# Which weight slices a recurrent loop streams, a copy in two parts, and one matmul group in another place

## The chip, the core and the metric

The kernel runs on one core of a Trainium2 chip. The metric is the device time of one execution in microseconds (us). All figures come from the profile and the trace of one profiled execution, or from the times of three further runs.

The engines, by the profile's names: PE does matmuls (PEld is its weight load), DVE and ACT are the vector and scalar engines, POOL is GpSimd, SP issues DMAs. ACT issues DMAs too. SBUF is the on-chip memory, PSUM holds what PE accumulates.

## The reference, cut to what matters

Two mixers read the same input x (2048 x 640) and a gate g adds them. A is a recurrent attention: x is cut into 64 segments of 32 rows, and each segment is joined with 8 memory rows that come out of the segment before it.

```python
for s in range(n_seg):                                  # 64 passes
    h = jnp.concatenate([mem, xs], axis=1)              # 8 + 32 rows, 640 wide
    q, k, v = (einsum('btd,dhe->bhte', h, W) for W in (Wq, Wk, Wv))   # 32 heads of 192
    p = softmax(where(mask, q @ k * scale, -1e9))
    o = einsum('bhte,hed->btd', p @ v, Wo)
    mem = o[:, :M, :]                                   # goes into the next pass
    outs.append(o[:, M:, :])
...
return g * a + (1 - g) * b
```

B is a local attention with a dilated window of 8 keys; it has its own projections. Each of Wq, Wk, Wv and Wo holds 640 x 6144 numbers in bf16, and every pass of A multiplies with all of them.

## The kernel before, in words

The work runs in four stages. Mixer B comes first (0 to about 190 us). The prepass (`prepass`, about 190 to 356 us) projects, for all 64 segments at once, the eight rows of x that the loop needs beside the memory, and writes them to a DRAM scratch. The loop (`part_a`, about 356 to 1660 us) makes the 64 passes, since the memory of one pass is an input of the next. `part_z` (to the end) finishes the remaining rows.

**Resident and streamed weights.** The four matrices do not all fit in SBUF. They are cut into slices of 384 KB. For Q, K and V a slice is named (matrix, u, kc): kc is one of five blocks of 128 rows of the 640, u one of three rounds of 512 columns, and it holds the columns of three of the four column groups (the fourth group is always resident). For Wo, "oa" is the first 384 output columns, in 12 slices, and "ob" the other 256, in 8 slices. `STREAM` (line 15) names the 14 slices that are not resident. They are copied once to a DRAM scratch `wscr`, and each pass reads all 14 from there, with `get_unit` (line 565), which issues the DMA of line 569 on SP. The tile pool of these slices, `wst`, has `WBUFS` = 5 buffers, which are used in turn. So the DMA of a slice is issued as soon as the last matmul with the slice five places before it has been done, and the slices come in the order in which the pass uses them. I write k03 for ("k", 0, 3), oa2 for ("oa", 2), and so on.

**Order in a pass.** The order of PE, ACT and DVE in the loop is written out by hand (a manual schedule, from line 956 on). `m_qk(i, kcs)` projects Q (i even) or K (i odd) of round i // 2 with the blocks kcs, `m_v(u, kcs)` projects V of round u (all at line 769); each block is four matmuls, one for each column group. `c_qk` copies a projection out of PSUM on ACT (line 782), `c_v(u)` copies V of round u on DVE into `VU[u]` (line 878). `t_qk` and `c_t` transpose. `s_a`, `s_b`, `e_exp`, `e_mask` (line 845), `e_norm` (line 855), `e_recip` make the softmax, for two halves h of the heads. `pv_half(h)` multiplies with V (lines 894 and, for the eight prepass rows `Vz`, 899); `Vz` is loaded in every pass by `load_vz` on ACT's queue (line 754). `c_x` and `c_z` copy the result (lines 908 and 915). `o_group(part, i2)` is one group of four matmuls with Wo (line 937); there are 12 groups of "oa" and 12 of "ob" in a pass.

`VU[1]` is columns 512 to 1024 of the tile `TZ`, while `pv_half` reads V in four tiles of 384 columns: `V[0]` 0 to 384, `V[1]` 384 to 768, `V[2]` 768 to 1152. So `pv_half(0)`, which reads `V[0]` and `V[1]`, needs `VU[0]` and the first half of `VU[1]`; the second half belongs to `V[2]` and is read by `pv_half(1)`.

**The end of a pass.** After `pv_half(1)` and its copies come six groups of ob (0 to 5), six of oa (6 to 11), a copy of the oa result on ACT (`whi`, line 1027), `load_z(s + 1)`, and six groups of ob (6 to 11). Behind ob group 8, `sel("oa", ...)` (line 948) multiplies that copy with a selection matrix, and DVE puts the result (line 951) into the next pass's `hT`, from which its first projection reads. So the next pass waits for the chain: last oa group, `whi`, `sel`, `hT`.

Of the kernel before, what the change touches and what calls it, by code (L numbers as in the profile page):

```python
# [11 lines left out]
F32 = mybir.dt.float32  # L12
I32 = mybir.dt.int32

STREAM = (("k", 0, 0), ("k", 0, 3), ("k", 1, 0), ("q", 2, 1), ("q", 2, 3), ("k", 2, 4), ("v", 0, 1), ("v", 1, 1), ("v", 2, 2),
          ("oa", 0), ("ob", 0), ("oa", 2), ("oa", 8), ("ob", 7))
N_EARLY = 21
N_COPY = 4
N_MID = 4
N_V = 8  # L20
# [2 lines left out]
WBUFS = 5  # L23
# [6 lines left out]
class _K:  # L30
# [463 lines left out]
    def units(self, m, J, kc):  # L494
        return [u for u in range(3) if J == 3 or (m, u, kc) not in STREAM]

    def weights_setup(self):
        nc, tc, KC = self.nc, self.tc, self.KC
        rest = []
        for m in "qkv":  # L500
            ks = sorted(range(KC), key=lambda kc: (len(self.units(m, 0, kc)) < 3, kc)) if m == "k" else range(KC)
            rest += [(m, J, kc) for kc in ks for J in range(4)]
        rest += [k for k in [("oa", i) for i in range(12)] + [("ob", i) for i in range(8)] if k not in STREAM]
        n = (0, N_EARLY, -N_MID - N_V - N_LAST, -N_V - N_LAST, -N_LAST, None)
        self.early, *self.late = [rest[n[x]:n[x + 1]] for x in range(5)]
# [5 lines left out]
        self.wstream = self.ctx.enter_context(tc.tile_pool(name="wstream", bufs=WBUFS))  # L511
        self.wscr = dict(zip(STREAM, self.dram.tile([len(STREAM), 128, 1536], BF, name="wscr")))

# [58 lines left out]
    def load_early(self):  # L572

        loads = [lambda k=k: self.load_res(k, self.tile_of(self.wres, k)) for k in self.early]
        self.pre_q = {}
        self.pre_keys = sorted((k for k in STREAM if k[0] in ("q", "k")), key=lambda k: (k[0] != "q", k[1]))
        loads += [lambda k=k: self.pre_q.update({k: self.load_unit(k)}) for k in self.pre_keys[:WBUFS]]
        loads += [lambda k=k: self.copy_unit(k) for k in STREAM[:N_COPY]]
        return loads
# [10 lines left out]
    def prepass(self):  # L590

        nc, tc, KC = self.nc, self.tc, self.KC
        nseg = self.S // self.seg
        NZ = nseg * 8
        self.zpk_dram = self.dram.tile([nseg, 128, 1152], BF, name="zpk_dram")

        def project_qk(p, pool):
            m, Rp = "qqkk"[p], p % 2
            ZS = pool.tile([128, nseg, 192], BF, name="ZS")
            if p == 2:  # L600
                for k in self.pre_keys[WBUFS:]:
                    self.pre_q[k] = self.load_unit(k)
            sts = {k: t for k, t in self.pre_q.items() if k[0] == m and k[1] in (2 * Rp, 1)}

            def weights(j, kc, l):
                key = (m, l // 4, kc)
                if j < 3 and key in sts:
                    return sts[key][:, 512 * j + 128 * (l % 4):512 * j + 128 * (l % 4) + 128]
                return self.res(m, j, kc, 128 * l, 128)

            if p == 2:
                for k in STREAM[N_COPY:]:
                    self.copy_unit(k)
            if p == 3:
                self.load_late(1)
            z0 = 768 + 192 * (1 - Rp) if m == "q" else 384 + 192 * Rp
            for r in range(2):
                for j in range(4):
                    for t in range(3):
                        ps = self.pst([128, NZ], F32, name="ps_pre")  # L620
                        for kc in range(KC):
                            nc.tensor.matmul(ps[:], lhsT=weights(j, kc, 6 * Rp + 3 * r + t), rhs=zTi[:, kc, :],  # L622
                                             start=(kc == 0), stop=(kc == KC - 1))
                        zc = 96 * r + 8 * (4 * t + j)
                        self.evac(ZS[:, :, zc:zc + 8], ps[:].rearrange("p (i s) -> p s i", i=8))
                        if p == 0 and 12 * r + 3 * j + t >= 6 and self.tail_outs:
                            self.tail_outs.pop(0)()
            nc.scalar.dma_start(self.zpk_dram[:, :, z0:z0 + 192].rearrange("s p f -> p s f"), ZS[:])

        vkeys = [k for k in STREAM if k[0] == "v"]  # L630

        def load_v(J):
            t = self.wstream.tile([128, 1536], BF, name="wst", tag="wst")
            for x, (m, u, kc) in enumerate(vkeys):
                nc.sync.dma_start(t[:, 512 * x:512 * x + 512],
                                  self.W["v"][:, kc, 1536 * J + 512 * u:1536 * J + 512 * u + 512])
            return t

        def project_v(vt, J):

            def weights(kc, g):
                if J < 3 and ("v", g, kc) in vkeys:
                    x = vkeys.index(("v", g, kc))
                    return vt[:, 512 * x:512 * x + 512]
                return self.res("v", J, kc, 512 * g, 512)

            for st in range(NZ // 128):
                ZV = zvp.tile([128, 1536], BF, name="ZV")
                pss = [self.pst([128, 512], F32, name="ps_pre") for _ in range(3)]
                for kc in range(KC):  # L650
                    for g in range(3):
                        mm = nc.tensor.matmul(pss[g][:], lhsT=zTi[:, kc, 128 * st:128 * st + 128],  # L652
                                         rhs=weights(kc, g), start=(kc == 0),
                                         stop=(kc == KC - 1))
                if 4 * J + st >= 3 and loads:
                    tc.add_manual_dep(loads.pop(0)().ins, mm.ins.name, self.after, reason="a load per tile")
                for g in range(3):
                    self.evac(ZV[:, 512 * g:512 * g + 512], pss[g][:])
                for k in range(2 * st, 2 * st + 2):
                    dst = self.zpk_dram[:, 32 * J + k:32 * J + 32:8, 0:384]  # L660
                    nc.scalar.dma_start(dst, ZV[64 * (k % 2):64 * (k % 2) + 64, :].rearrange("s (j f) -> s j f", j=4))

        zTi = self.zTi
        with ExitStack() as zc1:
            with tc.tile_pool(name="pre_zs0", bufs=1, reuse_waits="tile") as zs0:
                project_qk(0, zs0)
                self.out_ctx.close()
                zs1 = zc1.enter_context(tc.tile_pool(name="pre_zs1", bufs=1, side="right", reuse_waits="tile"))
                project_qk(1, zs1)
                project_qk(2, zs0)  # L670
            project_qk(3, zs1)
        vs = [load_v(J) for J in range(3)]
        loads = self.load_late(2, "right", wait=True)
        with tc.tile_pool(name="pre_zv", bufs=ZVB, reuse_waits="tile") as zvp:
            for J in range(4):
                project_v(vs[J] if J < 3 else None, J)
        for k in STREAM[:WBUFS]:
            self.ahead[k] = self.get_unit(k)

# [38 lines left out]
    def part_a(self):  # L718
        nc, tc, KC, S = self.nc, self.tc, self.KC, self.S
# [3 lines left out]
        with ctx:  # L723
# [3 lines left out]
            VU = [self.TZ[:, 512 * u:512 * u + 512] for u in range(3)]  # L727
# [33 lines left out]
            for s in range(nseg):  # L761
# [108 lines left out]
                pvs = {}  # L870
# [4 lines left out]
                    project(pvs[u], "v", u, kcs)  # L875

                def c_v(u):
                    nc.vector.tensor_copy(VU[u], pvs[u][:])  # L878

                def pv_half(h):  # L880
                    E = Es[h]
# [61 lines left out]
                def sel(part, hT_next, pm):  # L943

                    m0, m1 = (0, 3) if part == "oa" else (3, KC)
                    p = 0 if part == "oa" else 1
                    for m in range(m0, m1):
                        nc.tensor.matmul(pm[:, p, 8 * (m - m0):8 * (m - m0) + 8], lhsT=whi[:, m * 128:(m + 1) * 128],  # L948
                                         rhs=self.sel_m[:], start=(m == m0), stop=(m == m1 - 1),
                                         skip_group_check=True)  # L950
                    nc.vector.tensor_copy(hT_next[:, m0:m1, 0:8], pm[:, p, 0:8 * (m1 - m0)].rearrange(  # L951
                        "p (m i) -> p m i", i=8))
# [32 lines left out]
                e_mask(0)  # L985
                m_v(0)
                c_v(0)
                if s + 1 < nseg:
                    hT_next = self.load_seg(s + 1)
# [30 lines left out]
                nc.scalar.dma_start(self.oz_dram[s], zst)  # L1020
                if s + 1 == nseg:
                    self.sort_oz(0)
                for i2 in range(6):
                    o_group("ob", i2)
                for i2 in range(6, 12):
                    o_group("oa", i2)
# [1 line left out]
                if s + 1 < nseg:  # L1028
                    load_z(s + 1)
                    pm = psS.tile([128, 2, 512], F32, tag="S", name="ps_mem")  # L1030
                for i2 in range(6, 12):
                    o_group("ob", i2)
                    if i2 == 8 and s + 1 < nseg:
                        sel("oa", hT_next, pm)
# [135 lines left out]
```

## Time and profile before

| what | us |
|---|---|
| median of three runs (lowest, highest) | 1726.15 (1721.16, 1727.09) |
| the profiled execution, its own time | 1727.22 |
| its span in the trace | 1725.5 |
| PE busy in the span | 1608.7 |
| loop, 356 to 1660 us: PE busy of 1304 us | 1234.65 |
| from the first `c_v` of one pass to that of the next: mean of 63 | 20.41 |
| the same, shortest and longest | 19.25, 23.36 |

The granted clock of PE was 0.987 over the span. The times are to be read as one execution's: the work of a pass is the same in all 64 passes, so what differs between a pass of 19.25 us and one of 21 us is waiting. A matmul of the loop's projections has a mean duration of 380 ns in the list of groups, but such matmuls overlap, and four of them (one block) start every 206 to 216 ns; a wait of PE is therefore best read from the starts.

### The profile page before, as it was taken

What the parts mean: (1) busy time and instruction counts of PE and PEld (TensorE: products, weight loads), DVE (VectorE), ACT (ScalarE), POOL (GpSimd) and SP (SyncE); (2) the same over time, 40 slices, a digit from 0 to 9 for tenths busy, and PEclk for the clock granted to TensorE, in tenths of its full rate; (3) what the DMA queues carried; (4) which work ended last, traced back from release to release, by engine and by line L of the source; (5) the groups of instructions that cost most, each with busy time, mean ns of one, the idle gap of its engine ahead of it and who ended that gap; (6) DMA issues with size and microseconds to landing.
All of it is one profiled execution on the core that took longest, in us unless ns stands there. A gap on an engine that the chain in (4) does not pass through costs nothing.

```text
span 1725.5 us, 75561 instructions
## 1 busy us (share of the span) xinstructions
PE 1608.7 (93%) x33193; PEld 893.1 (52%) x33209; DVE 693.0 (40%) x2095; ACT 805.3 (47%) x2082; POOL 59.8 (3%) x124
## 2 busy tenths in 40 slices
PE   7887999999999999999999999999999999999989
PEld 4545544445555555555555555555555555555557
DVE  3666333234443343344443343444333443434430
ACT  3877322234444444444444444454444444444450
POOL 2030000000000000000000000000000000000000
PEclk9999899999999999999999999999999999999999
DMA  7888798989998998899999998999999998999981
GB/s 196 199 208 210 233 325 212 266 273 295 298 306 299 311 318 292 285 294 296 293 295 306 309 315 291 289 307 303 301 298 306 291 302 283 294 292 294 298 288 31
DMA packets 306391, 479.04 MB, mean 278 GB/s; under 512 B 100492, under 2 KB 184460, under 8 KB 306060
## 3 DMA queue, kind: packets, MB, share of 16 engines
q1 hardware_dynamic: 206928, 417.73, 75.1%
q10 hardware_dynamic: 99132, 56.46, 11.4%
q8 instruction: 260, 4.26, 1.0%
q14 instruction: 71, 0.58, 0.1%
HBM read 432.37 MB, written 47.23 MB: 278 GB/s over the span
## 4 chain that ended last, share of the span: by engine, by line
PE 71%; DMA 21%; ACT 2%; issue 2%; SPq 1%; DVE 1%; ACTq 0%; DVEq 0%
PE ps_qk L769 17%; DMA wst<-wscr 15%; PE ps_v L769 11%; PE ps_wo L937 11%; PE ps_pre L622 6%; PE ps_qkT L790 5%; PE ps_S L823 4%; PE ps_oT L894 4%; PE ps_pre L652 3%; PE ps_z L1101 2%; DMA TZ<-zpk_dram 2%; PE ps_S L855 2%; PE ps_bqk L236 1%; DMA bqkT<-bqk_dram 1%; PE ps_bo L360 1%
## 5 line engine op out<-in xcount | busy, mean ns | idle before, releaser
L769 PEld LDWEIGHTS <-hT 128*32 128x32 bf16 x11520 | 280.6, 96 | 311.8 <-issue 45.2
L782 ACT CAST TZ<-ps_qk 128x512 bf16<-128x512 f32 x384 | 219.7, 586 | 348.4 <-PE ps_qk L769 344.1
L769 PE MATMUL ps_qk<-w_q,hT 128*32 128x512 bf16 x3456 | 272.8, 382 | 1.5 <-issue 1.5
L769 PE MATMUL ps_qk<-w_k,hT 128*32 128x512 bf16 x3072 | 262.6, 380 | 0.0
L801 DVE COPY ZB<-ps_qkT 128x512 bf16<-128x512 bf16 (+1 forms) x256 | 90.9, 355 | 384.6 <-PE ps_qkT L790 284.2
L769 PE MATMUL ps_v<-w_v,hT 128*32 128x512 bf16 x3264 | 242.1, 381 | 0.0
L937 PEld LDWEIGHTS <-TZ 128*32 128x32 bf16 x6144 | 149.1, 96 | 94.5 <-ACT TZ L908 33.4
L769 PE MATMUL ps_qk<-wst,hT 128*32 128x512 bf16 x1152 | 150.0, 381 | 25.6 <-DMA wst<-wscr 24.2
L878 DVE CAST TZ<-ps_v 128x512 bf16<-128x512 f32 x192 | 132.8, 691 | 37.4 <-PE ps_v L769 37.3
L937 PE MATMUL ps_wo<-w_oa,TZ 128*32 128x384 bf16 x2304 | 136.6, 330 | 6.4 <-issue 5.0
L908 ACT CAST TZ<-ps_oT 128x192 bf16<-128x192 f32 x256 | 75.8, 322 | 136.6 <-PE ps_oT L899 76.0
L937 PE MATMUL ps_wo<-wst,TZ 128*32 128x384 bf16 (+1 forms) x1536 | 127.6, 306 | 2.5 <-issue 1.6
L937 PE MATMUL ps_wo<-w_ob,TZ 128*32 128x256 bf16 x2304 | 107.0, 274 | 9.0 <-issue 8.8
L908 DVE CAST TZ<-ps_oT 128x192 bf16<-128x192 f32 x256 | 85.7, 355 | 71.4 <-PE ps_oT L899 69.6
L951 DVE CAST hT<-ps_mem 128x24 bf16<-128x24 f32 x126 | 22.5, 178 | 216.3 <-PE ps_mem L948 216.3
L790 PE MATMUL ps_qkT<-ident,TZ 128*128 128x128 bf16 x1536 | 108.2, 221 | 0.0
L790 PEld LDWEIGHTS <-TZ 128*128 128x128 bf16 x1536 | 89.3, 98 | 21.6 <-issue 21.6
L841 ACT ACTIVATE TZ<-ps_S 32x224 bf16<-32x224 f32 x256 | 89.0, 348 | 9.6
L841 ACT ACTIVATE ZB<-ps_S 32x224 bf16<-32x224 f32 x256 | 89.0, 348 | 8.8
L750 POOL COPY TZ<-ZB 128x384 bf16<-128x384 bf16 x64 | 32.5, 507 | 1492.8 <-DMA ZB<-zpk_dram 783.5
L823 PE MATMUL ps_S<-ZB,TZ 64*128 64x160 bf16 (+1 forms) x768 | 82.2, 233 | 0.0
L894 PEld LDWEIGHTS <-TZ 32*128 32x128 bf16 (+1 forms) x4096 | 46.9, 97 | 63.0 <-issue 27.1
(133 smaller groups left out, 2042.6 us busy)
## 6 DMA issues: line engine op xcount, KB each, us to landing
wst<-wscr SPq DMA_DIRECT2D x896, 384.0 KB
zpk_dram<-ZS ACTq DMA_DIRECT2D x4, 3072.0 KB
ZB<-zpk_dram ACTq DMA_DIRECT2D x64, 192.0 KB
zpk_dram<-ZV ACTq DMA_DIRECT2D x32, 192.0 KB
TZ<-zpk_dram ACTq DMA_DIRECT2D x64, 96.0 KB
oz_dram<-TZ ACTq DMA_DIRECT2D x64, 96.0 KB
w_q<-in_A_Wq_dram SPq DMA_DIRECT2D x14, 384.0 KB
w_v<-in_A_Wv_dram SPq DMA_DIRECT2D x14, 384.0 KB
```

The lines of the kernel that those rows point to most:

```text
L622: nc.tensor.matmul(ps[:], lhsT=weights(j, kc, 6 * Rp + 3 * r + t), rhs=zTi[:, kc, :], start=(kc == 0), stop=(kc == KC - 1))
L652: mm = nc.tensor.matmul(pss[g][:], lhsT=zTi[:, kc, 128 * st:128 * st + 128], rhs=weights(kc, g), start=(kc == 0), stop=(kc == KC - 1))
L769: nc.tensor.matmul(ps[32 * j:32 * j + 32, :], lhsT=hT[:, kc, :], rhs=rhs, start=(kc == 0), stop=(kc == KC - 1), tile_position=(0, 32 * j), ...
L782: nc.scalar.copy(sts[i], pqs[i][:])
L790: nc.tensor.transpose(pT[:, 128 * t:128 * t + 128], st[:, 128 * t:128 * t + 128], self.ident[:])
L801: nc.vector.tensor_copy(QTf[:, run[2]:run[2] + 4, run[3]:run[3] + n, :].rearrange("p b x i -> p x b i"), src.rearrange("p (x b i) -> p x b ...
L823: nc.tensor.matmul(grid(h, par)[:, :, 0:80].rearrange("p j (b r i) -> p j b r i", r=2, i=8)[:, :, :, r, :], lhsT=KTs[3 * R + t][k0:k1, :], ...
L841: nc.scalar.activation(E[ps], pSs[h][ps, :, 112 * j:112 * j + 112], ACT.Exp, scale=scale_a)
L878: nc.vector.tensor_copy(VU[u], pvs[u][:])
L894: nc.tensor.matmul(out[:, r, t, :], lhsT=V[2 * h + r][ks, f0:f1], rhs=E[ks, par, 0:80].rearrange("p (b r i) -> p b r i", r=2, i=8)[:, :, r ...
L908: cp(oTxs[2 * h + j // 2][:, 6 * (j % 2):6 * (j % 2) + 6, :], pos[j][:, 0:240].rearrange("p (c q) -> p c q", q=40)[:, :, 8:40])
L937: nc.tensor.matmul(pso[part][32 * jj:32 * jj + 32, 0:n], lhsT=oTxs[2 * (g // 2) + J // 2][:, 6 * (J % 2) + 3 * (g % 2) + t, :], rhs=osl[pa ...
```

## The change

Three edits in the loop, and what follows from them ahead of it.

1. `STREAM` names other slices: ten of Q, K, V and four of Wo, where it was nine and five. The size of what a pass streams, 14 slices of 384 KB, and the five buffers stay. One more resident slice of Q, K, V or Wo is loaded early (`N_EARLY` 22 for 21). With four streamed slices of V instead of three, the prepass loads V's streamed columns in two tiles for each column group (`load_v`), one of three slices and one of one: six tiles in all, five ahead and the sixth after the first group has been projected.
2. `c_v(1)` copies `VU[1]` in two parts of 256 columns.
3. ob group 5 moves from ahead of oa groups 6 to 11 to behind them (and behind `whi` and `load_z`).

```diff
-STREAM = (("k", 0, 0), ("k", 0, 3), ("k", 1, 0), ("q", 2, 1), ("q", 2, 3), ("k", 2, 4), ("v", 0, 1), ("v", 1, 1), ("v", 2, 2),
-          ("oa", 0), ("ob", 0), ("oa", 2), ("oa", 8), ("ob", 7))
-N_EARLY = 21
+STREAM = (("k", 0, 2), ("q", 1, 1), ("k", 1, 2), ("q", 2, 1), ("q", 2, 4), ("k", 2, 4), ("v", 0, 0), ("v", 1, 0), ("v", 1, 3),
+          ("v", 2, 2), ("oa", 0), ("ob", 0), ("oa", 5), ("ob", 7))
+N_EARLY = 22
...
-        def load_v(J):
+        def load_v(J, n):
             t = self.wstream.tile([128, 1536], BF, name="wst", tag="wst")
-            for x, (m, u, kc) in enumerate(vkeys):
+            for x, (m, u, kc) in enumerate(vkeys[3 * n:3 * n + 3]):
...
-        vs = [load_v(J) for J in range(3)]
+        vs = [(J, n) for J in range(3) for n in range((len(vkeys) + 2) // 3)]
+        vts = [load_v(*v) for v in vs[:WBUFS]]
...
             for J in range(4):
-                project_v(vs[J] if J < 3 else None, J)
+                project_v([t for v, t in zip(vs, vts) if v[0] == J], J)
+                vts += [load_v(*v) for v in vs[len(vts):]]
...
                 def c_v(u):
-                    nc.vector.tensor_copy(VU[u], pvs[u][:])
+                    for f0, f1 in ((0, 256), (256, 512)) if u == 1 else ((0, 512),):
+                        nc.vector.tensor_copy(VU[u][:, f0:f1], pvs[u][:, f0:f1])
...
-                for i2 in range(6):
+                for i2 in range(5):
                     o_group("ob", i2)
                 for i2 in range(6, 12):
                     o_group("oa", i2)
...
-                for i2 in range(6, 12):
+                for i2 in range(5, 12):
                     o_group("ob", i2)
                     if i2 == 8 and s + 1 < nseg:
                         sel("oa", hT_next, pm)
```

More of the change, by code (lines that the diff above doesn't have):

```diff
@@ L643, in weights @@
                     x = vkeys.index(("v", g, kc))
-                    return vt[:, 512 * x:512 * x + 512]
+                    return vt[x // 3][:, 512 * (x % 3):512 * (x % 3) + 512]
                 return self.res("v", J, kc, 512 * g, 512)
```

## The prediction

> **What bounds the kernel.** I read the page's engine shares first, then the loop's windows, then PE's waits in the loop, then single passes in the timeline.
>
> ```profile
> PE 1608.7 (93%) x33193; PEld 893.1 (52%) x33209; DVE 693.0 (40%) x2095; ACT 805.3 (47%) x2082; POOL 59.8 (3%) x124
> ...
> q1 hardware_dynamic: 206928, 417.73, 75.1%
> ```
>
> PE is busy almost throughout, and q1, SP's queue with the streamed slices, takes three quarters of the DMA engines' time. Either could be the bound, so passes have to be compared.
>
> ```profile
> 551.83:571.08 19.25, 18.98 (x449) 10.56 (x445) 8.23 (x29) 9.71 (x28) 0.51 (x1) 1.00 0.92 314
> 390.14:1653.00 1262.86, 1199.58 (x27594) 661.87 (x27590) 511.21 (x1737) 603.01 (x1736) 31.44 (x62) 1.00 0.91 299
> ```
>
> These are the windows of one short pass and of 62 passes (length, busy time of PE, PEld, DVE, ACT, POOL, clock, DMA share, GB/s). The short pass takes 19.25 us at 314 GB/s, the mean pass 20.37 us at 299 GB/s with the same work. So the transfers can go faster than they do on average, and some 1.1 us of a mean pass is waiting. PE's waits in the loop say for what (us in total, times, longest):
>
> ```profile
> PE ps_qk L769 <- DMA wst<-wscr: 24.2, 35, 2.0
> ...
> PE ps_mem L948 <- ACT ZB L1027: 14.7, 57, 0.5
> ...
> PE ps_oT L899 <- DMA TZ<-zpk_dram: 1.4, 5, 0.4
> ```
>
> The first row is projections that wait for a streamed slice, the second the selection that waits for the copy `whi`. Each row counts only idle time after the modelled end of the matmul before. That end is 379 ns after its start, while the next block can start after 206, so each slice wait hides another 0.17 us: 24.2 + 35 x 0.17 = **30 us** for the slices.
>
> **Edit 1, other slices: -23 us.** A buffer is refilled when the slice five places before has been used, so a slice's lead is the time from that use to its own. I took the median gap between each two neighbouring PE starts of the 62 inner passes, which gives a pass without waits (19.22 us), and read from it when each slice is used. Before, the leads are in us: k00 5.3, k03 5.0, k10 5.8, q21 6.3, q23 6.8, k24 7.1, v01 7.4, v11 8.1, v22 8.2, oa0 8.1, ob0 8.6, oa2 7.5, oa8 6.0, ob7 5.8. Five uses (ob0, oa2, oa8, ob7, k00) lie 0.66 to 1.08 us apart, so five refills are issued almost at once. Packets of one slice take 1.05 us at best and 1.3 to 1.9 us in most places, so these refills queue up: from issue to first packet it is about 0.8 to 1.7 us at k00, k03, k10 and oa8, but 2.3 at q21 and 3.2 at k24. Placing each wait by its slice (start over the usual 206 ns), q21 waits in 26 passes for 15 us, k03 in 12 for 7, k10 in 7 for 6.5, q23 in 4 and k24 in 3 for 2.5 and 1.7 us; the slices with leads from 7.4 us up hardly at all.
>
> With the new list, the same pass without waits gives: k02 7.5, q11 7.4, k12 6.95, q21 6.9, q24 7.0, k24 6.4, v00 6.55, v10 6.35, v13 7.3, v22 6.4, oa0 6.8, ob0 7.0, oa5 6.8, ob7 6.7. The shortest lead grows from 5.0 to 6.35 us, and no more than two uses in a row are under 1 us apart (0.86 to 0.88), so the queue stays at about one slice. Such slices resemble the old oa8 and ob7 (leads 6.0 and 5.8, short queue: one wait in 62 passes and none) more than the old q21. I take one wait of 0.5 us in 62 passes for each of 14 slices, 7 us, so 30 - 7 = 23 us go. Bounds: all 30 go, or (as at k24, with a lead of 7.1 and a long queue) 3 waits of 0.57 for each of 14, 24 us, and only 6 go.
>
> Outside the loop this edit adds three loads of 128 KB in the prepass and one early load of 384 KB. In the prepass PE runs matmul after matmul (107.7 us busy of 110 between 190 and 300 us), and none of its waits there is for these tiles. The sixth V tile is loaded on SP behind the first column group, some 20 us ahead of its use; behind it on SP stand Wo loads and the refills for the loop, which have 12 us of the last group as cover. I cost it at nothing; without the cover it is 0.8 MB at 273 GB/s, 3 us.
>
> **Edit 2, the copy in two: -7 us.** One pass in the timeline:
>
> ```profile
> 901.25 0.69 DVE L878 CAST TZ<-ps_v 128x512 bf16<-128x512 f32 x1 [0.62 <-PE ps_v L769]
> ...
> 901.78 0.42 PE L894 MATMUL ps_oT<-TZ 32*128 32x40 bf16 x16
> 901.86 0.27 DVE L845 TENSOR_TENSOR ZB<-ZB,mask 128x224 bf16<-128x224 bf16 x1
> ...
> 902.39 0.28 PE L855 MATMUL ps_S<-ZB,bones 128*32 128x160 bf16 x8
> ```
>
> The 16 matmuls of L894 are one group on the page's line, but their starts have a hole: twelve from 901.78 to 901.86, the last four (columns 640 to 768, of `VU[1]`) at 902.00, which is 901.94, the copy's end, and 0.06 us. Over all passes this hole is 147 ns where the neighbours have 15 to 29. The slope between the 192-column copy of L908 (355 ns) and the 512-column one (691 ns) is 1.05 ns a column, so half the columns take 267 ns less, and the first half ends about 424 ns after its start, at 901.67, before PE comes. So about 0.12 us a pass goes. What else becomes late: `e_mask` stands behind the copy on DVE. The next instruction starts 0.61 us after a 512-column copy, so 0.08 us of the 0.69 overlaps; two halves then hold DVE for 2 x (424 - 80) = 688 ns, 78 more. The mask would end at 902.21 instead of 902.13, and L855, which needs it, would come at 902.27 instead of 902.39: just in time with 0.06 us for the signal. 64 x 0.12 = 7.7 us, bounds 8.4 (all of 0.13) and 3 (the mask is late by 0.07).
>
> [...]
>
> **Edit 3, ob group 5 behind: -5 us.**
>
> ```profile
> 907.22 0.51 PE L937 MATMUL ps_wo<-w_ob,TZ 128*32 128x256 bf16 x12
> ...
> 907.45 0.48 ACT L1027 CAST ZB<-ps_wo 128x384 bf16<-128x384 f32 x1 [1.44 <-PE ps_wo L937]
> ...
> 907.99 0.23 PE L948 MATMUL ps_mem<-sel_m,ZB 128*128 128x8 bf16 x3 [0.26 <-ACT ZB L1027]
> ```
>
> After the three ob groups PE waits for `whi`: from the last group's start to L948 it is 528 ns in the median, where an ordinary change of this kind takes about 100 to 310. An ob group takes 108 ns (starts of neighbouring groups). Put into this wait it is free, and the chain from oa's end on starts 108 ns earlier. Ahead of oa 6, however, one cover group is missing: oa 6 reads the first ACT copy of `c_x(1)`, which ended at 905.29 in this pass; oa 6 started at 905.40 and now wants 905.29, and would be released at about 905.34. So 0.06 to 0.11 us a pass; 63 x 0.08 = 5 us, bounds 3.5 and 6.8. No DMA is moved past another by it; `load_z` is issued 0.1 us earlier.
>
> **Vz: +3 us.** `load_vz` is issued about 9.0 us into the pass on ACT's queue, and its packets run from 10.4 to 12.2. Before, refills are issued at 8.15 and 9.9 us; after, at 8.15, 9.7 and 10.8. One more slice shares the DMA engines then, and PE comes 0.12 us sooner. The waits for it now are short (row above); I take 0.05 us a pass, between nothing and a whole slice later (below).
>
> **Sum.** 1727.22 (the profiled execution, 1.1 us above the median of the three runs) - 23 - 7.7 - 5 + 3 = 1694.5, so **1694 us**, a pass of 19.9 us at some 307 GB/s.
>
> **Rivals.**
> - *The transfers are the bound:* waits move to other slices and what PE gains is waited for. For it: q1 at 75%, 0.91 DMA share. Against: passes at 314 and 317 GB/s, and old slices with long leads that hardly wait. It would give the loop's 299 GB/s again, 1727 us; half of it (24 us of slice waits left) 1712. Chance of over 1718 by it: 10%.
> - *Slower: Vz comes late.* Its last packet now ends about 1.2 us ahead of its use in the mean, and the signal takes most of the rest. If the extra slice delays it by one slice's 1.05 us, PE stands some 0.9 us in each pass at L899: 64 x 0.9 = 58, so 1694 - 3 + 58 = 1749 us. It decides from about 0.55 us a pass on, which eats the gain of 36. Against: packets of both queues take turns, and Vz is a quarter of a slice. Chance 8%.
> - *The split does nothing:* if PE's wait covers both parts, the second part ends 78 ns later: 64 x 0.08 = 5 us lost instead of 7.7 won, 1707 us. Against: the first twelve matmuls already pass the copy in flight. Chance 8%.
>
> The forecast itself has 74%. **Range:** from all waits gone and both other edits in full (30 + 8.4 + 6.8 = 45, 1682, and 3 us of run spread: 1679) to edit 1 at its low bound with edits 2 and 3 at theirs (6 + 3 + 3.5 = 12: 1715). Under 0.5% (9 us) a measurement of this kernel hardly tells from no change; chances: faster 0.82, within 0.5% 0.09, slower 0.09.
>
> **What would show it.** The row of L769 waiting for wst falls from 24.2 to about 6 us, and q21 no longer leads it; the hole in L894 falls from 147 to about 30 ns; the gap ahead of L948 by about 0.1 us; L899's wait for Vz stays under 6 us. If the wst waits stay over 18 us, or L899 waits in most passes, the prediction is wrong.

## The result, and the profile after

The changed kernel takes 1711.22 us in the median of 8 runs (1706.65 to 1718.71), the kernel before 1725.36 us (8 runs, 1719.9 to 1730.27): a ratio of **0.9922, with a 95% interval of 0.9898 to 0.9945**. It is faster by 14 us, where 33 us were forecast. The profiled execution took 1710.89 us, its span is 1709.1 us. Behind `STREAM` the lines of the changed kernel carry numbers that are 2 or 3 higher: L769 is now L771, L878 L881, L899 L902, L937 L940, L948 L951, L1027 L1030.

The page's engine shares and DMA queues, after (packets, MB, share of 16 engines):

```profile
PE 1602.0 (94%) x33193; PEld 888.6 (52%) x33209; DVE 697.0 (41%) x2159; ACT 803.7 (47%) x2082; POOL 60.0 (4%) x124
...
q1 hardware_dynamic: 208144, 418.12, 75.3%
...
q8 instruction: 260, 4.26, 1.0%
```

DVE has 64 instructions more, one more copy a pass, and q1 has the same share as before. The row to remember is the last, q8, which the prediction did not use: 260 packets of 16 KB, of the kind "instruction". The window of 62 inner passes, columns as in the prediction:

```profile
394.52:1635.91 1241.39, 1189.53 (x27594) 650.03 (x27590) 515.35 (x1799) 601.61 (x1736) 31.59 (x62) 1.00 0.92 304
```

The same 27,594 matmuls in 62 passes now take 1241.39 us, 20.02 a pass where 20.37 stood, at 304 GB/s for 299. PE's waits in the loop (us in total, times, longest), after:

```profile
PE ps_wo L940 <- issue: 21.2, 24, 1.8
PE ps_oT L902 <- DMA TZ<-zpk_dram: 11.5, 13, 1.5
PE ps_v L771 <- DMA wst<-wscr: 8.9, 2, 5.4
PE ps_qk L771 <- issue: 3.2, 4, 2.1
PE ps_oT L897 <- issue: 3.1, 8, 1.0
...
PE ps_mem L951 <- ACT ZB L1030: 1.2, 8, 0.2
...
PE ps_qk L771 <- DMA wst<-wscr: 0.4, 1, 0.4
```

and rows of the same view of before that the prediction did not show:

```profile
PE ps_wo L937 <- issue: 15.5, 19, 1.7
...
PE ps_v L769 <- DMA wst<-wscr: 5.1, 2, 2.6
...
PE ps_qk L769 <- issue: 1.5, 3, 1.0
```

Read them as a balance. The slices' row has gone, from 24.2 us to 0.4. The selection's wait for `whi` has gone, from 14.7 to 1.2. But the wait for `Vz` rose from 1.4 to 11.5, the rows "issue" together from 17.7 to 29.2, and the first pass's wait for a slice of V from 5.1 to 8.9. "issue" is time in which PE waits for nothing that the profile shows, neither a semaphore nor a result.

To put sizes on it I took, as in the prediction, the median gap between neighbouring PE starts as a pass without waits, and put each gap's excess (above 0.05 us) down to the wait that stands there. So hidden parts are included:

| us | before | after |
|---|---|---|
| a pass without waits | 19.22 | 19.01 |
| mean inner pass | 20.36 | 20.02 |
| waits for slices, 62 passes | 33.8 | 0.6 |
| waits for `Vz` | 2.6 | 15.0 |
| waits put down to issue | 23.6 | 37.6 |
| the first pass | 20.9 | 24.9 |

Over the 62 passes: edits 2 and 3 -13.4 (62 x 0.216), slices -33.2, `Vz` +12.4, issue +14.0, other gaps -1.1, together -21.3 us; the first pass gives 4 us back, and the loop starts 1.3 us later.

Edits 2 and 3 in one pass of the timeline, after:

```profile
894.52 0.76 DVE L881 CAST TZ<-ps_v 128x256 bf16<-128x256 f32 x2 [0.62 <-PE ps_v L771]
...
895.05 0.27 PE L897 MATMUL ps_oT<-TZ 32*128 32x40 bf16 x16
...
895.19 0.27 DVE L847 TENSOR_TENSOR ZB<-ZB,mask 128x224 bf16<-128x224 bf16 x1
...
895.51 0.28 PE L857 MATMUL ps_S<-ZB,bones 128*32 128x160 bf16 x8
...
900.97 0.51 PE L940 MATMUL ps_wo<-w_oa,TZ 128*32 128x384 bf16 x8 [1.68 <-issue]
...
901.52 0.48 ACT L1030 CAST ZB<-ps_wo 128x384 bf16<-128x384 f32 x1 [2.40 <-PE ps_wo L940]
...
902.06 0.23 PE L951 MATMUL ps_mem<-sel_m,ZB 128*128 128x8 bf16 x3
```

From the first matmul of L897 to L857 it is now 0.46 us, where L894 to L855 had 0.61. The median hole in the sixteen matmuls fell from 147 to 15 ns. The two copies hold DVE from 894.52 to 895.19, 0.67 us for 0.61. In the second half of the lines PE stands 1.68 us at L940 with all its operands there. That is an issue wait, and `whi` and the selection come later by it.

The first pass, SP's queue and PE's long wait, after, in rows of two answers of the timeline:

```profile
361.69 4.92 SPq L524 DMA_DIRECT2D w_ob<-in_A_Wo_dram  x4
366.67 8.39 SPq L569 DMA_DIRECT2D wst<-wscr  x6
```

```profile
374.09 0.62 PE L771 MATMUL ps_v<-wst,hT 128*32 128x512 bf16 x3 [5.44 <-DMA wst<-wscr]
```

The refill for a slice of V, `v10`, is issued at 366.67 behind four Wo loads. PE wants it about 368.6 and gets it at 374.09. The kernel before has four such loads in the same place (issued from 361.34 on), and its waits for V add up to 5.1 us.

### The profile page after: what moved, and what is told of

It is laid out like the page before. It is cut to its first block, busy times and chain, and to the rows that moved or that the text cites. A ratio compares the mean times of both kernels' runs of the same rounds, so it can differ in the third digit from the quotient of the medians.

```text
span 1709.1 us, 75634 instructions
## 1 busy us (share of the span) xinstructions
PE 1602.0 (94%) x33193; PEld 888.6 (52%) x33209; DVE 697.0 (41%) x2159; ACT 803.7 (47%) x2082; POOL 60.0 (4%) x124
## 4 chain that ended last, share of the span: by engine, by line
PE 81%; DMA 11%; ACT 3%; issue 3%; DVE 1%; SPq 1%; ACTq 0%; DVEq 0%
PE ps_qk L771 25%; PE ps_wo L940 13%; PE ps_v L771 10%; PE ps_pre L622 6%; DMA TZ<-zpk_dram 5%; PE ps_qkT L792 5%; PE ps_S L825 4%; PE ps_oT L897 3%; PE ps_z L1104 3%; PE ps_pre L652 3%; DMA wst<-wscr 2%; ACT ZB L1030 2%; PE ps_bqk L236 1%; PE ps_S L857 1%; PE ps_mem L951 1%
## 5 line engine op out<-in xcount | busy, mean ns | idle before, releaser
L771 PEld LDWEIGHTS <-hT 128*32 128x32 bf16 x11520 | 275.3, 96 | 284.5 <-issue 15.3
L771 PE MATMUL ps_qk<-w_q,hT 128*32 128x512 bf16 x3264 | 267.7, 383 | 2.8 <-issue 2.8
L771 PE MATMUL ps_qk<-w_k,hT 128*32 128x512 bf16 x3264 | 265.5, 380 | 0.7 <-DVE ZV L81 0.4
L771 PE MATMUL ps_v<-w_v,hT 128*32 128x512 bf16 x3072 | 243.7, 383 | 0.0
L940 PEld LDWEIGHTS <-TZ 128*32 128x32 bf16 x6144 | 145.7, 96 | 105.8 <-ACT TZ L911 41.6
L940 PE MATMUL ps_wo<-w_oa,TZ 128*32 128x384 bf16 x2560 | 148.2, 330 | 10.4 <-issue 9.8
L881 DVE CAST TZ<-ps_v 128x512 bf16<-128x512 f32 (+1 forms) x256 | 137.0, 556 | 43.8 <-PE ps_v L771 43.7
L771 PE MATMUL ps_qk<-wst,hT 128*32 128x512 bf16 x1152 | 149.1, 381 | 0.5 <-DMA wst<-wscr 0.4
L940 PE MATMUL ps_wo<-w_ob,TZ 128*32 128x256 bf16 x2304 | 107.2, 274 | 8.8 <-issue 8.7
L771 PE MATMUL ps_v<-wst,hT 128*32 128x512 bf16 x768 | 100.1, 385 | 8.9 <-DMA wst<-wscr 8.9
L940 PE MATMUL ps_wo<-wst,TZ 128*32 128x256 bf16 (+1 forms) x1280 | 96.3, 301 | 3.3 <-issue 2.7
```

The lines of the kernel that those rows point to most:

```text
L771: nc.tensor.matmul(ps[32 * j:32 * j + 32, :], lhsT=hT[:, kc, :], rhs=rhs, start=(kc == 0), stop=(kc == KC - 1), tile_position=(0, 32 * j), ...
L881: nc.vector.tensor_copy(VU[u][:, f0:f1], pvs[u][:, f0:f1])
L940: nc.tensor.matmul(pso[part][32 * jj:32 * jj + 32, 0:n], lhsT=oTxs[2 * (g // 2) + J // 2][:, 6 * (J % 2) + 3 * (g % 2) + t, :], rhs=osl[pa ...
```

## Experiments

Every ratio below is to the kernel before, run beside the experiment (medians of 1718.84 to 1719.7 us).

**The theory after the result: the waits were displaced.** Edit 1 removes the slices' waits, but an even stream takes the stretch in which the DMA engines had room for `Vz` and for PE's code, so most of its gain comes back as other waits; edits 2 and 3 give what was forecast. **Rivals:** that edit 1 gave the 14 us while the time won by edits 2 and 3 is waited for again; and, for the waits themselves, that the total load of the DMA engines makes them, not the place of the refills in the pass.

**1. Edit 1 alone** (the changed kernel without the other two):

```diff
-                    for f0, f1 in ((0, 256), (256, 512)) if u == 1 else ((0, 512),):
-                        nc.vector.tensor_copy(VU[u][:, f0:f1], pvs[u][:, f0:f1])
+                    nc.vector.tensor_copy(VU[u], pvs[u][:])
...
-                for i2 in range(5):
+                for i2 in range(6):
...
-                for i2 in range(5, 12):
+                for i2 in range(6, 12):
```

> Edit 1 alone (the new slices), edits 2 and 3 undone. Theory A (displaced waits: evening out the refills ends the waits for slices, but the DMA engines then have no slack stretch left in which the Vz load and PE's code loads ran, so those come late): PE's waits for slices in the loop fall from 29 to about 9 us (those 9 in the first pass), waits for Vz rise from 1.4 to about 9, waits put down to issue from 18 to about 28, and since both rows hide part of each wait the time stays near the kernel before: 1724 us (1716 to 1728). Theory B (the new waits come from PE reaching them sooner, by edits 2 and 3): Vz and issue stay at 1.4 and 18, and the time falls by the 30 us of slice waits less 4 in the first pass: 1697 us.

1721.0 us against 1718.91 for before: ratio 1.0014 (0.999 to 1.0038). PE's waits in its loop:

```profile
PE ps_wo L939 <- issue: 29.0, 23, 2.9
...
PE ps_oT L901 <- DMA TZ<-zpk_dram: 9.0, 14, 1.5
...
PE ps_qk L771 <- DMA wst<-wscr: 1.2, 1, 1.2
```

The slices' waits are gone beside the first pass, and the time has not moved. The rows "issue" add up to 40.2 us; this profiled execution, 1729.12 us, was the longest of its 12, so the size is on the high side. A pass without waits takes 19.20 us, as before. The displaced waits were borne out: this edit by itself is worth nothing.

**2. Edits 2 and 3 alone** (the kernel before with them; `STREAM`, `N_EARLY` and `load_v` stay):

```diff
-                    nc.vector.tensor_copy(VU[u], pvs[u][:])
+                    for f0, f1 in ((0, 256), (256, 512)) if u == 1 else ((0, 512),):
+                        nc.vector.tensor_copy(VU[u][:, f0:f1], pvs[u][:, f0:f1])
...
-                for i2 in range(6):
+                for i2 in range(5):
...
-                for i2 in range(6, 12):
+                for i2 in range(5, 12):
```

> Edits 2 and 3 alone (the copy in two, ob group 5 behind), with the old slices. Theory A: a pass without waits is 0.22 us shorter, as in the changed kernel (19.01 against 19.22 us), the waits for slices stay at 29 to 35 us, Vz stays under 4 and issue near 18: 1713 us (1708 to 1718). Theory B: Vz and issue rise as in the changed kernel, by 10 and 11 us of their rows, and take the gain away: 1725 to 1735 us.

1703.97 us, ratio 0.9925 (0.9897 to 0.9952), which is 12.9 us. A pass without waits takes 19.04 us. Its waits:

```profile
PE ps_qk L769 <- DMA wst<-wscr: 19.7, 40, 1.5
PE ps_wo L938 <- issue: 9.5, 17, 1.2
...
PE ps_oT L900 <- DMA TZ<-zpk_dram: 2.4, 6, 0.8
```

The slices' waits are still there, and the gain as well. The whole gain of the change is that of these two edits.

**3 and 4. Both kernels without refills.** In the loop each use takes one of the five tiles loaded ahead, so 384 KB x 14 a pass are not transferred and the matmuls read other weights (the rest of the edit sets up the list `fixed`):

```diff
...
-            return self.ahead.pop(key)
+            self.fixed.append(self.ahead.pop(key))
+            return self.fixed[-1]
+        if len(self.fixed) == WBUFS:
+            return self.fixed[STREAM.index(key) % WBUFS]
```

> The kernel before without any refill in the loop: the five slices loaded ahead of the loop are used in place of all 14 in every pass, so PE does the same matmuls on other numbers and SP's queue is empty in the loop. Both theories: no waits for slices, and a pass without waits of 19.22 us. Theory A: with the stream gone the waits for Vz go and those put down to issue fall from 18 to under 6 us: 1680 us (1672 to 1688). Theory B: issue stays at 18: 1692 us.

> The changed kernel without any refill in the loop, in the same way. Theory A: no waits for slices, for Vz or for code worth naming, a pass of 19.0 us; 13 to 14 us under the kernel before without refills (62 passes x 0.22): 1667 us (1659 to 1675). Theory B: Vz stays at 11 and issue at 28 us: about 1690 us.

1653.40 us, ratio 0.9622 (0.959 to 0.9655), and 1639.84 us, ratio 0.9548 (0.9515 to 0.9581). The difference, 13.6 us, was expected. Both levels came out 27 us lower than I had worked them out; the kernel before itself ran 8 us faster beside these runs (1718.91 us) than in its profile (1727.22). PE's waits, first before, then after, without refills:

```profile
PE ps_mem L951 <- ACT ZB L1030: 16.1, 63, 0.3
...
PE ps_wo L940 <- issue: 1.6, 4, 0.8
```

```profile
PE ps_wo L943 <- issue: 0.8, 2, 0.5
...
PE ps_mem L954 <- ACT ZB L1033: 0.2, 1, 0.2
```

The selection's wait goes from 16.1 to 0.2 us by the edits, with no stream beside them. The issue waits go from 17.7 and 29.2 us to 1.6 and 0.8 when the refills go: same program order on PE, same code to load, so the refills make them. The mean pass falls by 1.045 us in the kernel before, 64.8 us in 62 passes. The waits that I can name there are 60.0 (33.8 + 2.6 + 23.6). The other 4.8 us lie in gaps that I could not place, and the rest of the 27 us stays unexplained.

**5, 6 and 7. Which refills do it.** Three slices' refills carry only their first column block, and the matmuls reread that block; `SMALL` is (oa0, ob0, oa5), issued around `load_vz`; (k02, q11, k12), issued at its end and later in the pass; or (v10, v13, v22), issued ahead of it. That is 0.9, 0.77 and 0.77 MB less of 5.4 a pass.

```diff
-        self.nc.sync.dma_start(t[:], self.wscr[key])
+        n = 1536
+        if key in self.small:
+            n = {"oa": 384, "ob": 256}.get(key[0], 512)
+        self.nc.sync.dma_start(t[:, 0:n], self.wscr[key][:, 0:n])
...
-                                         rhs=osl[part, i][:, x, :],
+                                         rhs=osl[part, i][:, 0 if (part, i) in self.small else x, :],
```

> The changed kernel, but the refills of oa0, ob0 and oa5, which are issued at about 8.2, 9.7 and 10.8 us of a pass, carry only their first column block (a quarter, a sixth, a quarter of the bytes), and the matmuls with them read that block again and again: 2.3 slices of traffic less in each pass, PE's work the same on other numbers. Theory of place (the load of Vz is late because these refills run beside it; code loads are late because of the refills of a later stretch): PE's waits for Vz fall from 11.5 to under 3 us, waits put down to issue stay above 20 of 28: ratio to the kernel before 0.985 (0.980 to 0.988). Theory of total load (any 2 slices less help alike): Vz to about 7, issue to about 20.

> The same with k02, q11 and k12, whose refills are issued at about 13.5, 15.0 and 16.8 us of the pass before (a third of the bytes each: 2 slices less). Theory of place: waits put down to issue fall from 28 to under 14 us, since PE takes in its code fastest there, and Vz stays at 8 to 15: ratio 0.984 (0.979 to 0.988). Theory of total load: Vz to about 7, issue to about 20, ratio 0.987.

> The same with v10, v13 and v22, whose refills are issued at about 4.5, 5.3 and 7.1 us of a pass (2 slices less). Theory of place: issue stays above 24 us; Vz falls a little through the shorter queue ahead of it, to 5 to 10: ratio 0.989 (0.986 to 0.993). Theory of total load: as for the late three, 0.987.

Ratios: 0.9737 (0.971 to 0.9763), 0.9822 (0.9793 to 0.9851) and 0.9805 (0.9778 to 0.9833). The waits of the three, in this order; the first and the third have no row for `Vz`:

```profile
PE ps_wo L947 <- issue: 17.4, 21, 1.8
```

```profile
PE ps_oT L909 <- DMA TZ<-zpk_dram: 16.0, 16, 2.3
PE ps_wo L947 <- issue: 14.7, 20, 1.6
```

```profile
PE ps_wo L947 <- issue: 22.5, 27, 1.9
```

`Vz` is decided by place. Of the two equal amounts, 0.77 MB taken out ahead of it end its waits, and taken out later in the pass leave 16.0 us. So for `Vz` the total load by itself falls as a cause. The issue waits in all (rows of every line) are 18.3, 21.1 and 27.0 us, against 29.2 with full refills. By these numbers they answer more to the refills around and behind `load_vz` than to the early ones, but how much is not shown. My sizes were off: the first and the third gained more than expected, and the second left more issue waits than expected (21.1 for under 14). These are single profiles, and that of the second, 1701.54 us, was the longest of its five runs.

**8. A list with a gap.** All three edits, but with nine slices of Q, K, V and five of Wo, chosen so that the refills leave more of a gap around `load_vz`:

```diff
-STREAM = (("k", 0, 2), ("q", 1, 1), ("k", 1, 2), ("q", 2, 1), ("q", 2, 4), ("k", 2, 4), ("v", 0, 0), ("v", 1, 0), ("v", 1, 3),
-          ("v", 2, 2), ("oa", 0), ("ob", 0), ("oa", 5), ("ob", 7))
-N_EARLY = 22
+STREAM = (("k", 0, 2), ("q", 1, 1), ("k", 1, 2), ("q", 2, 1), ("q", 2, 4), ("k", 2, 4), ("v", 0, 1), ("v", 1, 1), ("v", 2, 2),
+          ("oa", 0), ("oa", 9), ("ob", 0), ("oa", 5), ("ob", 7))
+N_EARLY = 21
```

> All three edits, with another list: the new list's slices of Q and K, the old list's of V (v01, v11, v22), and oa0, oa9, ob0, oa5, ob7. Leads from 5.6 us (oa5) and 5.8 (ob7) to 8.2, those of the first six slices 6.0 to 7.0; refills at 8.2, 9.9 and 12.2 us around the load of Vz, as in the kernel before. Theory of place: Vz at 1 to 4 us as before, waits for slices under 8 us beside the first pass, issue 18 to 28: ratio 0.984 (0.979 to 0.989), under the changed kernel. Theory of total load: the waits come back elsewhere, 0.992.

1693.96 us, ratio **0.9866 (0.9842 to 0.9889)**. It beats the changed kernel, whose interval lies above. Its waits:

```profile
PE ps_wo L940 <- issue: 12.9, 19, 1.3
PE ps_qk L771 <- issue: 9.3, 10, 2.1
PE ps_v L771 <- DMA wst<-wscr: 6.5, 2, 3.5
PE ps_oT L902 <- DMA TZ<-zpk_dram: 5.7, 9, 2.0
```

`Vz` waits are half of those after (the expectation was lower still), issue 23.3 us in all for 29.2, the waits of Q's and K's projections for slices 0.4. Moving refills within the pass, with the load unchanged, gave 0.56% more than the change did.

**9. `Vz` loaded once** (in the first pass; later passes reuse it, so 63 loads of 96 KB and their data are left out):

```diff
-                load_vz(s)
+                if s == 0:
+                    load_vz(s)
```

> The changed kernel with Vz loaded in the first pass alone; later passes read what lies there, so the 96 KB and PE's waits for them are left out, and nothing else. If the late load of Vz costs what its row shows (11.5 us, with the hidden part some 15), the ratio falls from 0.992 to 0.984 (0.981 to 0.987), and the waits put down to issue stay at 20 to 30 us. If these waits only cover others (code loads that PE would meet next), the ratio stays above 0.989 and issue rises by about 10.

1696.03 us, ratio 0.9875 (0.9828 to 0.9923). The interval holds the first expectation and also the changed kernel's 0.9922, so the size of the gain is not settled. The waits:

```profile
PE ps_wo L940 <- issue: 27.1, 27, 2.2
...
PE ps_qk L771 <- issue: 3.8, 8, 0.8
```

No wait for `Vz` is left, and issue waits stand at 36.1 us for 29.2, 6.9 us more. That would fit one late load partly hiding another; with one profile each it is not shown.

**10 and 12. The first pass.** With the list of experiment 8 the Wo loads (`last_loads`) are issued further behind in the first pass, behind `m_v(0)` and `c_v(0)` in the one, behind `m_v(2, (0, 1, 2))` in the other:

```diff
...
-                if s == 0:
-                    for load in self.last_loads:
-                        load()
...
+                if s == 0:
+                    for load in self.last_loads:
+                        load()
```

> The mixed list with the last four resident loads of Wo issued in the first pass behind the projection of V round 0 instead of ahead of the refill of k24. If the first pass's waits for v01 (6.5 us in the mixed list) come from these loads standing ahead of the refills on SP's queue, the first pass is 4 to 7 us shorter and the ratio 0.983 (0.979 to 0.987). If they come from the refills' own lateness, nothing changes: 0.9866.

> The mixed list with the last four loads of Wo issued behind the refill of v22 in the first pass. In the run before they still stood third on SP's queue, ahead of the refill of v11, and V waited 6.5 us as before. If their place on that queue is the cause, V's waits for slices in the first pass fall from 6.5 to under 1.5 us and the first pass from 23.1 to about 18 us: about 5 us less than the mixed list, ratio 0.984 (0.980 to 0.988). If the refills are late for another reason, V still waits 5 us or more: 0.987.

1698.43 us, ratio 0.9888 (0.9857 to 0.992), and 1698.25, 0.9879 (0.9844 to 0.9914): neither is better than the list alone. In the first the Wo loads still stood third on SP's queue, ahead of a slice of V, and that slice was waited for as long as in experiment 8 (6.5 us). In the second one of the four still stood third there; the waits for V fell from 6.5 to 3.7 us, but Wo groups then waited 2.3 us for slices. The first pass took 23.1 us in experiment 8 and in the first of these, and 25.4 in the second. So neither run took all four loads out of the way of the refills, and both expectations were missed.

**11. Four buffers** (13 slices, chosen as evenly as in the change, with leads of 5.0 to 6.9 us; the edit of `STREAM` is named in the expectation):

```diff
...
-WBUFS = 5
+WBUFS = 4
```

> All three edits, four buffers and 13 streamed slices: k02, q11, k11, q21, q23, k24, v01, v11, v22, oa0, ob0, oa5, ob7; the room of the fifth buffer keeps one more slice resident. 7% fewer bytes are streamed, but the leads shrink to 5.0 (k24) to 6.8 us. If leads of 5.0 to 6 us are enough while the queue is short, as for the old oa8 and ob7, there are few waits for slices (under 8 us beside the first pass), and less traffic makes issue fall to 15 to 20: ratio 0.980 (0.975 to 0.985). If the lead itself decides, waits for slices come back with 25 us or more: ratio 0.992 or above.

1708.82 us, ratio 0.994 (0.9915 to 0.9965). Its waits:

```profile
PE ps_qk L771 <- DMA wst<-wscr: 20.7, 38, 1.6
PE ps_wo L940 <- issue: 17.5, 22, 1.9
```

The slices' waits are back at 20.7 us, and issue waits are lower with one slice fewer (18.9 in the rows of L940 and ps_qk L771, for 24.4). But the lead alone does not decide. In this run's median pass q21, q23, k24 and k11, with leads of 5.0 to 5.7 us, have all 55 waits for slices (counted from the starts), while oa5, ob7, q11 and k02, with 5.4 to 5.9, have none. In experiment 8 oa5, ob7 and k02 have such leads too, and PE waits 0.4 us for slices of Q and K and 0.2 for those of Wo. The last packet comes 3.6 to 3.9 us after issue in the mean at the first four and 3.3 to 3.5 at the others, so 1.3 to 1.9 us of the lead are left there and 2.1 to 2.5 here.

## Why the prediction was right in part, and where it failed

**Edit 1, the slices' waits: right, and more so.** Forecast 30 to 7 us, found 33.8 to 0.6. The leads of 6.35 us and more suffice in this list. The reason given, that a short queue makes leads of 6.0 and 5.8 us harmless as for the old oa8 and ob7, holds for the slices of Wo and not everywhere: in experiment 11 leads of 5.0 to 5.7 us brought 20.7 us of waits at four slices of Q and K.

**The sum of edit 1: the failed step.** The step "so 30 - 7 = 23 us go" took a slice's wait that goes as time won, and "the queue stays at about one slice" looked only at q1's own slices. Experiment 1 has edit 1 by itself: 23 us were forecast, and its ratio is 1.0014 (0.999 to 1.0038), so nothing was won. The 16 DMA engines also carry `Vz` (on q10, whose packets all together take 9.1% of their time between 340 and 1660 us before) and what I take for PE's code (q8, 1.1%), and those had lived from the uneven stream. Counted over a mean pass in steps of half a us, q1 keeps about 13 of the 16 engines busy in both kernels (13.0 and 13.1). But from 11 to 15.5 us after the pass's first projection all queues together kept 12.7 to 14.8 busy before and keep 14.7 to 15.8 now. The packets of `Vz` begin there at about 11 us: the last one comes 3.58 us after issue in the mean, for 3.12, while its use comes 4.14 us after issue in the median, for 4.29. In experiment 8 the same count falls to 11.6 at 13 us and to 10.4 at 14.5 us. Three terms came of it:

- **"Vz: +3 us" was mis-sized**: +12.4 in the passes, 0.2 us a pass instead of 0.05. The slower rival had the right mechanism at too high a price, 0.9 us a pass; the point from which it decides, 0.55, was not reached. Two of its steps stand in the traces: where PE waits for `Vz`, its last packet ends 0.68 us before PE starts in the median before and 0.65 after (6 and 16 waits over 0.05 us), over half of the 1.2 us named; and between the first and the last of its 128 packets q1 starts 119 packets in the mean before and 170 after, in turns with them (103 and 125 changes from one queue to the other). Experiments 5 to 7 show which refills make it.
- **Code loads were not in the sum**: +14.0 us (11.5 in the rows). The rows "issue" stood in the view of before with 17.7 us, and I passed them by as no affair of the change. That the refills make these waits is shown (experiments 3 and 4). That they are code loads rests on the records: q8's 260 packets of 16,384 bytes stand against 66,402 records of PE and PEld, 255 a packet. And PE starts again 1.1 to 1.6 us after the end of such a packet in all 41 issue waits after and all 25 before (those over 0.15 us), where only 8 to 9% of all PE starts in the loop lie in such a span. These waits take 29.2 us of PE's loop after, up to 2.1 us at once. Why a packet comes late is not in the trace, since it has no issue of these loads; one lasts 0.97 us in the median after and 1.03 without refills, so it would be a late start and not a slow packet.
- **The first pass, costed at nothing**, gives back 4 us. The named bound, 3 us without the cover, is near this by luck: it was reckoned from the added loads, and the long wait is for `v10`, whose refill stands behind four Wo loads that the kernel before has too. Two attempts to move these loads did not shorten the pass; why it is long stays open.

**Edits 2 and 3: right in mechanism and size.** Forecast 7.7 + 5 = 12.7 us. Found 12.9 by themselves, 13.6 without refills, 13.4 in the two profiles. The hole went by 0.13 us; the gap ahead of the selection fell from 528 to 421 ns, the 0.1 us named. The half copies take about 420 ns (424 forecast) and together hold DVE 65 ns longer than one (78 forecast): the mask starts 673 ns after the first of them in the median, where it started 608 ns after the one copy of 692 ns. No run has edit 2 or edit 3 alone. In the median pass the time from `pv_half(0)`'s first matmul to L855 (L857 after) fell from 610 to 460 ns, 9.3 us in 62 passes (7.7 forecast in 64 for edit 2), which leaves 4.1 for edit 3 (5 forecast).

**Rivals.** "The transfers are the bound" forecast 1712 us for its half, and 1711 came. Its direction was right, and the number is luck: it stood for 24 us of waits for slices, and 0.6 were left. Waits moved to other queues, not to other slices, and q1 was no fuller. So a place was lost, not throughput: with the same load, experiment 8 runs at 0.9866. "The split does nothing" fell, by the hole of 15 ns and by experiment 2. Of the signs named, one did miss: L899's wait for `Vz` was to stay under 6 us and came to 11.5. The two that were to show the prediction wrong did not catch this case: slices' waits are under 18 us, and `Vz` is late in 20 of 62 passes, not in most. Missing was a sign for the rows "issue".

**What stays open**: the long first pass, and how the issue waits divide between place and load, since each kernel has one profile and these rows differ by several us between kernels of like load.

## What to carry to other kernels

Before a stream's waits are counted as time won, list every other transfer on the same DMA engines, small loads and code among them, with issue, landing and use, and see whose stretch the new places take: here 33 us of waits went and some 30 came back elsewhere, 4 of them in the first pass. An even stream is no aim by itself; leave room around a small load that is needed soon after its issue, and set each slice's lead against the time from its issue to its last packet (6.4 us sufficed in the even list; in the old one q21 waited in 26 passes with 6.3). An edit on PE's own path can be proven by a pair of kernels without the stream, where the 13 us of these two edits stood out at once.

## What was not expected of the hardware

As far as the records tell, PE waits for its own code when the data stream fills the DMA engines, 17.7 us in the loop before, 29.2 after, 40.2 with edit 1 alone (in the longest of its 12 runs), and 0.8 to 1.6 without refills; in the profile it shows only as "issue" and in the queue "instruction", 1.0% of the engines' span. The DMA share of the loop hardly tells it: 0.91 and 0.92 with refills in the kernels before and after.
